# Moving DMA issues, logits order, a split softmax, a one-pass sum and one more tile addition in an attention and MLP kernel

## The chip, the core and the metric

The kernel runs on one core of a Trainium2 chip, in one launch. The metric is the device time of one execution in microseconds, as a median of several runs. A core has five engines with queues of their own: TensorE (PE; its weight loads are listed as PEld), VectorE (DVE), ScalarE (ACT), GpSimd (POOL) and SyncE (SP). Each takes its instructions in order and waits at semaphores. SP, ACT and POOL can issue DMAs, which 16 DMA engines carry out.

## What is computed

x has 2048 rows of 640 in bf16. The output is x plus an attention block plus an MLP, both on the same layer-normalised rows xn. The attention has 32 heads of 20; a row looks at itself and at the seven rows 2, 4, ..., 14 before it.

```python
def _A_ref(x, wqkv, wo):
    H = 32; Dh = D // H
    W, dil = 8, 2
    ...
    logits = jnp.einsum("bhsd,bhswd->bhsw", q, kg) * scale
    logits = jnp.where(mask[None, None, :, :], logits, -1e9)
    attn = _softmax(logits, axis=-1)
    o = jnp.einsum("bhsw,bhswd->bhsd", attn, vg)
    return (lambda x, *d: x.transpose(*d))(o, 0, 2, 1, 3).reshape(B, S, D) @ wo

def _B_ref(x, w1, b1, w2, b2):
    h = jnp.einsum("bsd,df->bsf", x, w1) + b1
    h = _gelu(h)
    return jnp.einsum("bsf,fd->bsd", h, w2) + b2

xn = _layernorm(x, axis=-1)
return x + _A_ref(xn, A_wqkv, A_wo) + _B_ref(xn, B_w1, B_b1, B_w2, B_b2)
```

## The kernel before

The rows are cut into four chunks of 512 (n = 0 to 3, NCH), each of four blocks of 128 (BPC). The 640 columns are five tiles of 128 (KT). Activations are held transposed: 128 columns on the partitions and 512 rows along the free side. The columns of wqkv are taken so that a head's 20 values lie in four neighbouring partitions across all five tiles.

The program is a list of small pieces. ORDER, written out by hand, says in which order they are put into the queues of PE, DVE, ACT and SP; the engines then run apart, held together only by semaphores. A name tells piece and chunk:

- `st`, `su`, `sq`, `rs`, `rc`, `xn`: statistics and normalisation; `tc`: the turn of xn into xnT, for chunks 1 to 3 a DMA transpose issued on SP.
- `pj{n}{which}{to}` and `pc`: projection of q, k or v, five matmuls into one of four psA buffers (L334), and the eviction of that buffer by ACT (L398). Chunk 0 does the same in pairs of blocks (`hj`, `hc`).
- `f1`, `ge`: first MLP product (L586, psA too) and GELU on ACT (L602).
- `qk{n}{pair}{h}`: on DVE, q times the four shifted k of one half h of the window, into the buffer half[h], 5120 elements a partition (L431).
- `pa` and `pb`: on DVE, additions among the five tiles of half[h] (2048 elements each, L463, L468), so that fewer tiles are left for PE. LEVEL[n] says how many: at 0 PE sums five tiles, at 1 tiles 0, 2 and 4, at 2 tiles 0 and 4.
- `lg{n}`: on PE, the sums over the 20 values of a head, one matmul for each tile left, half and block (L477), into the one PSUM tile L.
- `m`, `mx`, `ex`, `ss`, `ri`, `at`: the softmax over the window of eight. Maximum, subtraction, exponential (ACT), sum, reciprocal as exp(-ln) (ACT), product (DVE). ACT needs one table set for GELU and another for exp and ln, and `table` loads it when it changes.
- `xd{n}`, `xs{n}`: the expansion. Four DMAs copy the 32 head rows of each block's attn to the 128 partitions, 256 KB each (L550): blocks 0 and 1 issued on SP (`xd`), 2 and 3 on ACT (`xs`). Chunks 0 and 2 write to the tile ax, 1 and 3 to rows of x_sb that are spent.
- `av{n}{j}{h}`: on DVE, v times the expanded attn of block j, into half[h] (L565). `ad` and `ot` add the window up to oT (L574, L579).
- `t{n}{s}{pc}`: output products of chunks 0 to 2, transposed (L660); `t..4` reads oT. `u` evicts on ACT, `ut` turns the result back by a DMA transpose on SP, `ud` adds it to the output by a DMA from POOL. Chunk 3's products are not transposed (`o`, L621, L623; `o..4` reads oT) and go out by `oc` and `od`. `xp` writes x itself to the output first.
- `ldx`, `ld2`, `ldo`: the later loads on SP (x of chunks 2 and 3, w2, then wo and the broadcast bias b2bc).

The half buffers, L and the softmax tiles exist once. So qk of the next chunk waits until lg has read half, av too, and the next lg waits until the softmax has read L.

Of the kernel before, what the change touches and what calls it, by code (L numbers as in the profile page):

```python
# [30 lines left out]
WARM = 10  # L31
RB = 32
TURNED = 4

LEVEL = (1, 0, 1, 1)
ACT_STATS = (2, 3)

COLS = ((0, 2), (2, 4), (4, 5))

ORDER = """  # L40
pad01 pad02 st00a st00 sum1 rs00 mean1 neg1 sq1 xn00a xn00b tp00a wa tp00b wb tc00a tc00b rs01 ga xn01a xn01b gb2
tp01a gb3 tp01b tc01a tc01b gb4 gd gc0 ge tb b1 gc4 hj100 ho hj101 hj202 st03a st03 st02a st02 gc1 rs03 xn03 hj201
hc100 rs02 xn02 st11a st13a hc202 st10a st11 st12a hc201 tp03 tc03 tp02 tc02 hj200 hc200 hj102 hc102 hc101 hj012 st13
st10 st12 rs1 rc1 hj011 hc011 qk001 hj112 xn10 tc10 hc012 xn12 tc12 qk000 hj111 pa010 hc111 hj110 hc110 pk hc112 hj010
hc010 qk010 qk011 hj211 hc211 pa001 pa011 xn13 tc13 hj210 hc210 xn11 tc11 pa000 f10_10 hj212 hc212 pad12 f10_7 ge0_10
f10_0 f10_4 ge0_4 ge0_7 pad11 f10_6 ge0_6 pj102 pj112 pc102 pj100 ldx ld2 ldo ge0_0 pj103 lg0 mask pc103 pc112 pc100
pj114 su20 pc114 m0 mx0 ex0 pj110 pc110 pj101 pc101 pj111 ss0 pc111 pj113 ri0 at0 xd0 pc113 pj104 pc104 qk100 qk111
qk110 qk101 su21 f10_2 ge0_2 f10_8 ge0_8 xs0 f10_11 ge0_11 f10_1 ge0_1 f11_10 ge1_10 f11_7 ge1_7 f11_3 f11_0 su22
ge1_0 f10_9 f10_3 f10_5 lg1 av030 av020 m1 su23 ge0_9 ng2 sq22 xp0 ge1_3 sq23 ge0_5 sq21 ge0_3 f11_5 ge1_5 av021 sq20
t000 f11_9 ge1_9 rs2 rc2 xn21 tc21 xn20 tc20 mx1 t040 t041 xp1 t001 ex1 av000 pj120 pc120 xn22 tc22 pj122 pc122 av010  # L50
pj124 xn23 tc23 ss1 av011 av001 ri1 at1 xd1 pc124 pj123 av031 ad01 ad00 t042 t002 t003 f11_1 f11_2 pj121 t043 ad02 ot0
su30 pc123 pc121 av101 xs1 av120 av100 pj200 pc200 pj222 av110 av130 pc222 pj221 pc221 pj211 xp2 pc211 pj202 pc202
pj220 av121 pj212 pc220 pc212 pj214 pc214 av131 av111 pj201 pc201 su32 pj204 pc204 pj213 su33 su31 ng3 t004 t044 u00
f11_11 pc213 t010 ut00 t011 sq31 sq30 sq32 u04 sq33 rs3 rc3 t012 t013 t014 pj203 t020 u01 xn30 tc30 pc203 t021 t022
t023 t030 t031 t032 ad10 xn32 tc32 ut01 pj224 t033 ge1_1 xn33 tc33 ad11 ad12 t034 t024 pc224 pj210 xn31 tc31 pc210 ot1
pad21 f11_6 ge1_6 qk201 qk200 f12_4 pa210 ge2_4 ud00 ge1_2 u03 f11_4 ge1_4 pa200 ud01 f11_8 ge1_11 u02 pj302 t120
pj300 pc300 pj311 pc311 pc302 ge1_8 pj312 qk210 pj323 qk211 pa201 pc312 pad22 pj310 pc310 pad31 pa211 pj314 t121 pj301
t122 pc301 pc323 pj303 xl t123 pj304 pj313 lg2 pc313 f13_11 pc314 ut02 ut03 ut04 m2 mx2 pc303 pc304 ge3_11 qk311
f12_10 f12_11 ex2 t100 t101 ss2 ri2 pa311 ud02 at2 f12_7 ge2_10 t102 ge2_7 t124 qk300 t103 t104 xp3 ge2_11 u10 qk310
qk301 pj321 pc321 f13_8 ge3_8 f12_5 ge2_5 pj324 f12_6 xd2 ut10 ud10 pa300 t110 f13_3 t111 t112 pa310 t113 pc324 ge2_6  # L60
f13_0 f12_0 ge3_0 pa301 f12_8 lg3 m3 pj223 u12 ge3_3 mx3 f12_2 xs2 pc223 av201 ex3 t114 u11 ut11 ud11 ss3 ri3 t130
t131 t132 t133 f13_9 t140 t141 t142 ge2_0 av200 at3 ge2_8 av220 av230 xs3 t143 f12_1 ge2_1 t134 ud03 u13 pj320 ge2_2
t144 u14 t200 ut12 av211 av221 av210 av231 ad21 ut13 ad20 ad22 ot2 f13_1 ge3_1 pc320 pj322 pc322 pad32 av331 f12_9
f13_4 ge3_9 f13_5 ge3_5 f12_3 ge2_3 xd3 av311 ut14 f13_6 t201 t230 ud12 xb3 f13_10 t231 ge2_9 t202 t203 ud13 ge3_4
t232 t233 t234 u23 f13_2 t204 u20 ut20 t210 ud14 t211 t212 ud04 av320 f13_7 ud20 t213 ge3_7 t214 t220 t221 ge3_6 u21
t240 av330 t241 t222 t223 t224 t242 t243 u22 ut21 t244 ge3_2 ud21 ut22 ud22 ut23 ud23 o310 o311 o312 av310 ge3_10 o313
av321 av301 av300 ad31 ad30 u24 ut24 ad32 ot3 o320 o321 o322 o323 o324 oc32 o330 od32 o314 oc31 od31 o300 o301 o302
o303 o304 o331 o332 o333 o334 oc30 ohi ud24 oclo ochi ochd od30
""".split()


# [1 line left out]
def kernel(  # L73
# [396 lines left out]
    def do_lg(n):  # L470
        L = psL.tile([P, W, P], F32, tag="L", name="L")
        tiles["L", n] = L
        ts = (range(KT), (0, 2, 4), (0, 4), (0,))[LEVEL[n]]
        for t in ts:
            for h in range(2):
                for j in range(BPC):
                    nc.tensor.matmul(  # L477
                        L[j * H : (j + 1) * H, W // 2 * h : W // 2 * (h + 1), :],
                        lhsT=head_of[:],
                        rhs=half[h][:, :, t, j * P : (j + 1) * P],  # L480
                        start=(t == 0),
                        stop=(t == ts[-1]),
                        skip_group_check=True,
                    )
# [2 lines left out]
        L = tiles["L", 0]  # L487
        nc.vector.tensor_tensor(out=L[0:H, :, 0:MW], in0=L[0:H, :, 0:MW], in1=mask[:], op=ALU.add)

    def do_max(n):  # L490
        m = smp.tile([P, P], F32, tag="m", name="m")
        tiles["m", n] = m
        nc.vector.tensor_reduce(
            out=m[:], in_=tiles["L", n][:].rearrange("p w c -> p c w"), axis=AX.X, op=ALU.max
        )

    def do_sub(n):
        L = tiles["L", n]
        nc.vector.tensor_tensor(  # L499
            out=L[:],  # L500
            in0=L[:],
            in1=tiles["m", n][:].unsqueeze(1).to_broadcast([P, W, P]),
            op=ALU.subtract,
        )

    def do_exp(n):
        e = smp.tile([P, W, P], BF16, tag="e", name="e")
        tiles["e", n] = e
        table(LOG_SET)
        nc.scalar.activation(e[:], tiles["L", n][:], ACT.Exp, scale=SCALE)  # L510

    def do_sum(n):
        a = smp.tile([P, W // 2, P], F32, tag="sums", name="sums")
        tiles["ss", n] = a
        e = tiles["e", n]
        nc.vector.tensor_tensor(out=a[:], in0=e[:, 0 : W // 2, :], in1=e[:, W // 2 :, :], op=ALU.add)
        for k in (2, 1):
            nc.vector.tensor_tensor(out=a[:, 0:k, :], in0=a[:, 0:k, :], in1=a[:, k : 2 * k, :], op=ALU.add)

    def do_recip(n):  # L520
        rs = smp.tile([P, P], F32, tag="m", name="rs")
        tiles["rs", n] = rs
        total = tiles["ss", n][:, 0, :]
        table(LOG_SET)
        nc.scalar.activation(total, total, ACT.Ln)
        nc.scalar.activation(rs[:], total, ACT.Exp, scale=-1.0)

    def do_attn(n):
        attn = smp.tile([P, W, P], BF16, tag="attn", name="attn")
        tiles["attn", n] = attn  # L530
        nc.vector.tensor_tensor(  # L531
            out=attn[:],
            in0=tiles["e", n][:],
            in1=tiles["rs", n][:].unsqueeze(1).to_broadcast([P, W, P]),
            op=ALU.mult,
        )

# [18 lines left out]
        expand(nc.sync, n, (0, 1))  # L556

    def do_xs(n):
        expand(nc.scalar, n, (2, 3))


    def do_av(n, j, h):
# [173 lines left out]
    for n in range(NCH):  # L736
# [30 lines left out]
                piece(f"pb{n}{h}{t}", do_pb, n, h, t)  # L767
        piece(f"lg{n}", do_lg, n)
        for name, fn in (("m", do_max), ("mx", do_sub), ("ex", do_exp), ("ss", do_sum), ("ri", do_recip), ("at", do_attn)):
            piece(f"{name}{n}", fn, n)  # L770
        piece(f"xd{n}", do_xd, n)
        piece(f"xs{n}", do_xs, n)
        for k in range(3):
# [60 lines left out]
```

## Time and profile before

| What | Value |
|---|---|
| time, median of 3 runs | 211.18 us (211.13 to 211.46) |
| the profiled execution: its time | 211.18 us |
| its span in the trace | 209.0 us |
| PE busy | 203.0 us, 1162 matmuls recorded |
| DVE busy | 174.1 us, 141 instructions |
| ACT busy | 124.5 us, 229 instructions |
| POOL busy | 24.8 us |
| mean DMA traffic | 114 GB/s |

The span runs from the program's first instruction to its last; the rest of the time lies around it. Busy time is the union of an engine's instructions. A matmul of 512 columns is listed with 379 ns, but matmuls overlap, and in a row of them one starts every 0.216 us (20 in 4.32 us). "L477" is a line of the kernel. In a group's line the numbers are total busy time, mean ns of one, and the engine's idle time just before, with what ended it. A few matmul records are missing from the trace.

### The profile page before, as it was taken

Reading aid. Unit: us, or ns where it says so; the run is one execution under the profiler, and the core shown is the slowest. Engines: PE = TensorE matmul, PEld = TensorE weight load, DVE = VectorE, ACT = ScalarE, POOL = GpSimd, SP = SyncE. Lnnn points to the kernel's source line nnn. Section 1 sums busy time; section 2 is a strip of 40 time slices with the busy share of each in tenths; the row PEclk is TensorE's granted clock in tenths of the full one; section 3 lists DMA queues with packets and bytes.
Section 4 is the critical chain, followed back from the end, with each engine's and each line's share of the span. In section 5 each row is a group of like instructions: output and inputs, shape, how many; then the busy total and the mean of one; then the engine's idle time right before and its main releaser. Section 6 shows DMA issues by size and latency. Waiting matters only on the chain.

```text
span 209.0 us, 2962 instructions
## 1 busy us (share of the span) xinstructions
PE 203.0 (97%) x1162; PEld 107.1 (51%) x1180; DVE 174.1 (83%) x141; ACT 124.5 (60%) x229; POOL 24.8 (12%) x37
## 2 busy tenths in 40 slices
PE   8999999999999989999999999999999999999993
PEld 3999744544444445444455444444444444445552
DVE  3598996599699999999999879995999999997001
ACT  5579885988988557968765295814756502340210
POOL 2000000000000000020207000202042100225420
PEclk9999999999999999999999999999999999999999
DMA  6994379558006490135719302888189830548633
GB/s 213 387 396 137 68 225 395 226 80 239 13 8 185 79 297 11 25 25 75 104 33 94 25 3 92 127 95 122 32 132 140 80 28 19 56 50 91 56 46 63
DMA packets 36863, 23.88 MB, mean 114 GB/s; under 512 B 24946, under 2 KB 34674, under 8 KB 36850
## 3 DMA queue, kind: packets, MB, share of 16 engines
q1 hardware_dynamic: 25168, 16.65, 29.6%
q0 software_dynamic: 8752, 2.95, 17.5%
q10 hardware_dynamic: 2930, 4.10, 7.4%
q8 instruction: 9, 0.15, 0.3%
q14 instruction: 4, 0.03, 0.1%
HBM read 10.00 MB, written 5.57 MB: 74 GB/s over the span
## 4 chain that ended last, share of the span: by engine, by line
PE 88%; DVE 5%; ACT 2%; DMA 1%; ACTq 1%; issue 1%
PE T L660 24%; PE hps L586 24%; PE pps L334 20%; PE lo L621 7%; PE gps L378 7%; PE L L477 3%; DVE half L565 3%; PE hi L623 2%; PE gps L347 1%; DMA x_sb<-in_A_x_dram 1%; ACTq L550 1%; ACT L171 1%; DVE L L499 1%; DVE attn L531 1%; PE tp L278 0%
## 5 line engine op out<-in xcount | busy, mean ns | idle before, releaser
L586 PE MATMUL hps<-xnT,w_sb 128*128 128x512 bf16 x233 | 54.9, 379 | 0.4
L431 DVE TENSOR_TENSOR half<-qT,kT 128x5120 bf16<-128x5120 bf16 x16 | 44.3, 2818 | 0.0
L660 PE MATMUL T<-hT,w_sb 128*128 128x512 bf16 x179 | 42.7, 379 | 0.1
L672 POOL DMA_DIRECT2D out_dram<-x_sb x15 | 19.4, 1295 | 154.9 <-DMA x_sb<-x_sb 154.6
L586 PEld LDWEIGHTS <-w_sb 128*128 128x128 bf16 x240 | 23.3, 98 | 28.1 <-issue 0.8
L660 PEld LDWEIGHTS <-w_sb 128*128 128x128 bf16 x180 | 17.6, 98 | 21.1
L602 ACT ACTIVATE hT<-hps,bT 128x512 bf16<-128x512 f32 x36 | 23.6, 686 | 6.1 <-PE hps L586 6.0
L565 DVE TENSOR_TENSOR half<-vT,ax 128x2560 bf16<-128x2560 bf16 x16 | 23.1, 1483 | 2.0 <-PE L L477 2.0
L565 DVE TENSOR_TENSOR half<-vT,x_sb 128x2560 bf16<-128x2560 bf16 x16 | 22.6, 1483 | 0.0
L574 DVE TENSOR_TENSOR half<-half,half 128x5120 bf16<-128x5120 bf16 x8 | 22.2, 2822 | 0.1
L334 PE MATMUL pps<-xnT,wv_sb 128*128 128x512 bf16 x73 | 17.9, 379 | 0.9 <-ACT qT L398 0.8
L663 ACT ACTIVATE x_sb<-T,bT 128x512 bf16<-128x512 f32 x15 | 10.3, 685 | 14.0 <-PE T L660 13.0
L334 PE MATMUL pps<-xnT,wq_sb 128*128 128x512 bf16 x75 | 18.3, 379 | 0.0
L660 PE MATMUL T<-oT,wo 128*128 128x512 bf16 x73 | 18.2, 379 | 0.1
L334 PE MATMUL pps<-xnT,wk_sb 128*128 128x512 bf16 x72 | 17.7, 379 | 0.2
L463 DVE TENSOR_TENSOR half<-half 128x2048 bf16<-128x2048 bf16 x12 | 14.1, 1215 | 0.0
L398 ACT CAST qT<-pps 128x512 bf16<-128x512 f32 x15 | 8.7, 590 | 8.9 <-PE pps L334 8.9
L171 ACT ACT_TABLE_LOAD x10 | 12.8, 1283 | 0.9 <-PEq L818 0.7
L261 ACT ACTIVATE xn<-x_sb,nmr,rstd 128x640 bf16<-128x640 bf16 x12 | 11.0, 921 | 3.9 <-DVE nmr L251 2.2
L334 PEld LDWEIGHTS <-wv_sb 128*128 128x128 bf16 x75 | 8.7, 118 | 8.8 <-issue 1.5
L398 ACT CAST kT<-pps 128x512 bf16<-128x512 f32 x15 | 8.7, 587 | 7.3 <-PE pps L334 7.3
L334 PEld LDWEIGHTS <-wq_sb 128*128 128x128 bf16 x75 | 8.8, 117 | 7.5
(90 smaller groups left out, 231.5 us busy)
## 6 DMA issues: line engine op xcount, KB each, us to landing
w_sb<-in_B_w_dram SPq DMA_DIRECT2D x4, 960.0 KB, 10.2
out_dram<-x_sb POOLq DMA_DIRECT2D x15, 128.0 KB, 4.0
x_sb<-in_A_x_dram SPq DMA_DIRECT2D x1, 1280.0 KB, 6.2
out_dram<-x_sb ACTq DMA_DIRECT2D x2, 640.0 KB, 3.8
ax<-attn SPq DMA_DIRECT2D x4, 256.0 KB, 5.9
ax<-attn ACTq DMA_DIRECT2D x4, 256.0 KB, 6.0
x_sb<-attn SPq DMA_DIRECT2D x4, 256.0 KB, 4.7
x_sb<-attn ACTq DMA_DIRECT2D x4, 256.0 KB, 5.1
```

Of the source, the lines that this page charges most:

```text
L171: nc.scalar.preload_act_table_set(name)
L334: nc.tensor.matmul(ps[:], lhsT=wqkv_p[which][:, ti, to, :], rhs=xnT[:, ti, :], start=(ti == 0), stop=(ti == KT - 1),)
L378: nc.tensor.matmul(ps[:, to - a, :], lhsT=wqkv_p[which][:, ti, to, :], rhs=tiles["xnT", 0][:, ti, pair * 2 * P : (pair + 1) * 2 * P], star ...
L398: nc.scalar.copy(dest[:, to, off : off + CH], tiles["pps", n, which, to][:])
L431: nc.vector.tensor_tensor(out=half[h][:, :, :, cs], in0=q[:, :, at].unsqueeze(1).to_broadcast([P, W // 2, KT, 2 * P]), in1=window(k, h, at ...
L565: nc.vector.tensor_tensor(out=half[h][:, :, :, cs], in0=window(qkv_tile(n, 2), h, cs), in1=ax_view(n)[:, j, ws, :].unsqueeze(2).to_broadca ...
L574: nc.vector.tensor_tensor(out=a, in0=a, in1=b, op=ALU.add)
L586: nc.tensor.matmul(ps[:], lhsT=w1_sb[:, ti, ft * P : (ft + 1) * P], rhs=tiles["xnT", n][:, ti, :], start=(ti == 0), stop=(ti == KT - 1),)
L602: nc.scalar.activation(hT, tiles["hps", n, ft][:], ACT.Gelu_apprx_tanh, bias=bT[:, ft : ft + 1], scale=1.0)
L621: nc.tensor.matmul(lo[:], lhsT=lhs, rhs=rhs[:, 0:CH], start=first, stop=last)
L660: nc.tensor.matmul(ps[:], lhsT=lhs, rhs=rhs, start=pc == 0 and k == 0, stop=pc == 4 and k == len(srcs) - 1)
L672: nc.gpsimd.dma_start(dst, src, accum_op=ALU.add)
```

## The change

Five edits and a new ORDER.

- `xs` is issued on SP as well, so all four expansions of a chunk stand on one queue. In ORDER `ldo` and `xp0` come after `xd0` and ahead of `xs0`; in chunks 2 and 3 `xs` comes ahead of `xd`.
- `lg` runs over the halves outside and the tiles inside; it was the other way round.
- PARTS cuts chunk 0's softmax into two parts of 64 columns (`m0a`, `m0b` and so on). The subtraction of a part writes to the first bytes of half[0], in SBUF, not back to L.
- `ss` is one `tensor_reduce` over the window instead of three additions.
- LEVEL is 2 for chunks 2 and 3: two `pb` pieces each, and `lg` over tiles 0 and 4.

ORDER is new as a whole. It is shown where the pieces named here stand.

```diff
--- before.py
+++ after.py
@@ -31,41 +31,43 @@
 WARM = 10
 RB = 32
 TURNED = 4
-
-LEVEL = (1, 0, 1, 1)
+PARTS = (2, 1, 1, 1)
+
+LEVEL = (1, 0, 2, 2)
 ACT_STATS = (2, 3)
 
 COLS = ((0, 2), (2, 4), (4, 5))
 
 ORDER = """
...
-f10_0 f10_4 ge0_4 ge0_7 pad11 f10_6 ge0_6 pj102 pj112 pc102 pj100 ldx ld2 ldo ge0_0 pj103 lg0 mask pc103 pc112 pc100
-pj114 su20 pc114 m0 mx0 ex0 pj110 pc110 pj101 pc101 pj111 ss0 pc111 pj113 ri0 at0 xd0 pc113 pj104 pc104 qk100 qk111
-qk110 qk101 su21 f10_2 ge0_2 f10_8 ge0_8 xs0 f10_11 ge0_11 f10_1 ge0_1 f11_10 ge1_10 f11_7 ge1_7 f11_3 f11_0 su22
...
-pj124 xn23 tc23 ss1 av011 av001 ri1 at1 xd1 pc124 pj123 av031 ad01 ad00 t042 t002 t003 f11_1 f11_2 pj121 t043 ad02 ot0
-su30 pc123 pc121 av101 xs1 av120 av100 pj200 pc200 pj222 av110 av130 pc222 pj221 pc221 pj211 xp2 pc211 pj202 pc202
...
-t122 pc301 pc323 pj303 xl t123 pj304 pj313 lg2 pc313 f13_11 pc314 ut02 ut03 ut04 m2 mx2 pc303 pc304 ge3_11 qk311
-f12_10 f12_11 ex2 t100 t101 ss2 ri2 pa311 ud02 at2 f12_7 ge2_10 t102 ge2_7 t124 qk300 t103 t104 xp3 ge2_11 u10 qk310
-qk301 pj321 pc321 f13_8 ge3_8 f12_5 ge2_5 pj324 f12_6 xd2 ut10 ud10 pa300 t110 f13_3 t111 t112 pa310 t113 pc324 ge2_6
-f13_0 f12_0 ge3_0 pa301 f12_8 lg3 m3 pj223 u12 ge3_3 mx3 f12_2 xs2 pc223 av201 ex3 t114 u11 ut11 ud11 ss3 ri3 t130
...
+pj113 pc113 pj103 pj111 ge0_10 pj101 pc111 pj114 ldx ge0_7 pa000 pc101 pa010 lg0 mask m0a ld2 pc103 pj102 pc114 pad11
+su21 mx0a ex0a pj112 pc112 m0b mx0b ss0a pc102 ex0b ri0a ss0b pj100 pc100 at0a ri0b at0b pj110 pj104 pc104 pc110 xd0
+qk111 f10_2 ge0_2 su22 qk100 hj212 hc212 f10_6 ge0_6 pj121 su20 f10_1 pc121 su23 ldo f11_10 ge1_10 ng2 ge0_1 sq20
+f11_5 f10_11 pj122 pc122 f10_3 qk110 sq22 t040 qk101 f11_0 t000 lg1 xp0 av010 ge0_3 sq21 xs0 ge1_0 sq23 rs2 f10_8
+ge0_8 t001 m1 f11_3 rc2 xn23 tc23 ge0_11 av031 t041 mx1 av021 xn20 tc20 f11_7 av011 ge1_5 ge1_7 av001 ge1_3 xp1 f10_9
+t042 t002 xn21 ge0_9 tc21 pj120 xn22 tc22 av030 av000 f11_9 ge1_9 pj124 ex1 av020 ss1 pc120 pc124 pj123 pc123 ad00 ri1
+t043 f11_2 t003 pj204 at1 pc204 xd1 su31 ad01 pad12 ad02 ot0 pj200 pc200 pj201 pc201 av101 xp2 pj212 su30 pc212 pj220
...
+pj302 pc302 f13_6 ge3_6 pj323 lg2 pc312 qk300 m2 pc323 f11_11 ge1_11 f13_0 ge3_0 mx2 ut04 f13_11 ge3_9 ex2 pa300 ss2
+qk310 ri2 at2 xs2 qk301 t130 t131 f12_1 ge2_1 ge3_11 t132 f13_10 qk311 t102 t103 f13_2 pa310 xd2 t104 pj320 pc320
+f13_1 ge3_1 u10 ut10 ud10 f12_8 pa311 pa301 pb312 ge2_8 f13_8 ge3_8 t110 t133 t111 t112 t113 t114 u11 ge3_10 f12_5
+pj222 pc222 pj321 pc321 pb302 lg3 av200 t134 u13 m3 av221 ge2_5 xb3 f12_11 t140 t141 t120 ut11 mx3 f12_2 ge3_2 av211
...
 """.split()
@@ -471,8 +473,8 @@
         L = psL.tile([P, W, P], F32, tag="L", name="L")
         tiles["L", n] = L
         ts = (range(KT), (0, 2, 4), (0, 4), (0,))[LEVEL[n]]
-        for t in ts:
-            for h in range(2):
+        for h in range(2):
+            for t in ts:
                 for j in range(BPC):
                     nc.tensor.matmul(
                         L[j * H : (j + 1) * H, W // 2 * h : W // 2 * (h + 1), :],
@@ -487,51 +489,62 @@
         L = tiles["L", 0]
         nc.vector.tensor_tensor(out=L[0:H, :, 0:MW], in0=L[0:H, :, 0:MW], in1=mask[:], op=ALU.add)
 
-    def do_max(n):
-        m = smp.tile([P, P], F32, tag="m", name="m")
-        tiles["m", n] = m
+
+    def part(n, i):
+        width = P // PARTS[n]
+        return slice(i * width, (i + 1) * width), width
+
+    def softmax_tile(key, n, shape, dtype):
+        return get((key, n), lambda: smp.tile([P, PARTS[n]] + [s // PARTS[n] if s == P else s for s in shape], dtype, tag=key, name=key))
+
+    def shifted(n, i):
+        cs, width = part(n, i)
+        if PARTS[n] == 1:
+            return tiles["L", n][:]
+        low = half[0][:].rearrange("p w t c -> p (w t c)").bitcast(F32)[:, 0 : W * P]
+        return low.rearrange("p (i w c) -> p i w c", i=PARTS[n], w=W)[:, i, :, :]
+
+    def do_max(n, i):
+        cs, width = part(n, i)
+        m = softmax_tile("m", n, [P], F32)
         nc.vector.tensor_reduce(
-            out=m[:], in_=tiles["L", n][:].rearrange("p w c -> p c w"), axis=AX.X, op=ALU.max
-        )
-
-    def do_sub(n):
-        L = tiles["L", n]
+            out=m[:, i, :], in_=tiles["L", n][:, :, cs].rearrange("p w c -> p c w"), axis=AX.X, op=ALU.max
+        )
+
+    def do_sub(n, i):
+        cs, width = part(n, i)
         nc.vector.tensor_tensor(
-            out=L[:],
-            in0=L[:],
-            in1=tiles["m", n][:].unsqueeze(1).to_broadcast([P, W, P]),
+            out=shifted(n, i),
+            in0=tiles["L", n][:, :, cs],
+            in1=tiles["m", n][:, i, :].unsqueeze(1).to_broadcast([P, W, width]),
             op=ALU.subtract,
         )
 
-    def do_exp(n):
-        e = smp.tile([P, W, P], BF16, tag="e", name="e")
-        tiles["e", n] = e
+    def do_exp(n, i):
+        e = softmax_tile("e", n, [W, P], BF16)
         table(LOG_SET)
-        nc.scalar.activation(e[:], tiles["L", n][:], ACT.Exp, scale=SCALE)
-
-    def do_sum(n):
-        a = smp.tile([P, W // 2, P], F32, tag="sums", name="sums")
-        tiles["ss", n] = a
-        e = tiles["e", n]
-        nc.vector.tensor_tensor(out=a[:], in0=e[:, 0 : W // 2, :], in1=e[:, W // 2 :, :], op=ALU.add)
-        for k in (2, 1):
-            nc.vector.tensor_tensor(out=a[:, 0:k, :], in0=a[:, 0:k, :], in1=a[:, k : 2 * k, :], op=ALU.add)
-
-    def do_recip(n):
-        rs = smp.tile([P, P], F32, tag="m", name="rs")
-        tiles["rs", n] = rs
-        total = tiles["ss", n][:, 0, :]
+        nc.scalar.activation(e[:, i, :, :], shifted(n, i), ACT.Exp, scale=SCALE)
+
+    def do_sum(n, i):
+        total = softmax_tile("sums", n, [P], F32)
+        nc.vector.tensor_reduce(
+            out=total[:, i, :], in_=tiles["e", n][:, i, :, :].rearrange("p w c -> p c w"), axis=AX.X, op=ALU.add
+        )
+
+    def do_recip(n, i):
+        rs = get(("rs", n), lambda: smp.tile([P, PARTS[n], P // PARTS[n]], F32, tag="m", name="rs"))
+        total = tiles["sums", n][:, i, :]
         table(LOG_SET)
         nc.scalar.activation(total, total, ACT.Ln)
-        nc.scalar.activation(rs[:], total, ACT.Exp, scale=-1.0)
-
-    def do_attn(n):
-        attn = smp.tile([P, W, P], BF16, tag="attn", name="attn")
-        tiles["attn", n] = attn
+        nc.scalar.activation(rs[:, i, :], total, ACT.Exp, scale=-1.0)
+
+    def do_attn(n, i):
+        cs, width = part(n, i)
+        attn = get(("attn", n), lambda: smp.tile([P, W, P], BF16, tag="attn", name="attn"))
         nc.vector.tensor_tensor(
-            out=attn[:],
-            in0=tiles["e", n][:],
-            in1=tiles["rs", n][:].unsqueeze(1).to_broadcast([P, W, P]),
+            out=attn[:, :, cs],
+            in0=tiles["e", n][:, i, :, :],
+            in1=tiles["rs", n][:, i, :].unsqueeze(1).to_broadcast([P, W, width]),
             op=ALU.mult,
         )
 
@@ -556,7 +569,7 @@
         expand(nc.sync, n, (0, 1))
 
     def do_xs(n):
-        expand(nc.scalar, n, (2, 3))
+        expand(nc.sync, n, (2, 3))
 
 
     def do_av(n, j, h):
@@ -767,7 +780,8 @@
                 piece(f"pb{n}{h}{t}", do_pb, n, h, t)
         piece(f"lg{n}", do_lg, n)
         for name, fn in (("m", do_max), ("mx", do_sub), ("ex", do_exp), ("ss", do_sum), ("ri", do_recip), ("at", do_attn)):
-            piece(f"{name}{n}", fn, n)
+            for i in range(PARTS[n]):
+                piece(f"{name}{n}" + ("" if PARTS[n] == 1 else "ab"[i]), fn, n, i)
         piece(f"xd{n}", do_xd, n)
         piece(f"xs{n}", do_xs, n)
         for k in range(3):
```

## The prediction

> **What bounds the kernel now.** I read the page first (busy shares, 40 slices, the chain that ended last), then PE's waits, the chain in order of time around each logits block, the timeline around PE's one wait, and VectorE's groups with the shapes kept apart.
>
> ```profile
> PE 203.0 (97%) x1162; PEld 107.1 (51%) x1180; DVE 174.1 (83%) x141; ACT 124.5 (60%) x229; POOL 24.8 (12%) x37
> PEclk9999999999999999999999999999999999999999
> DMA  6994379558006490135719302888189830548633
> PE 88%; DVE 5%; ACT 2%; DMA 1%; ACTq 1%; issue 1%
> ```
>
> PE is busy 97% of the span at full granted clock, and 88% of the last chain is PE. Its matmuls start 0.216 us apart (20 hps matmuls in 4.32 us on the chain), so this is work, not waiting. A change pays only if it takes matmuls away from PE or closes a hole in PE, and it costs only where it opens one. There is one hole after the start:
>
> ```profile
> PE pps L334 <- ACT qT L398: 0.8, 1, 0.8
> ```
>
> That is PE's list of waits; its place in the timeline (start, us, engine, line; idle before it in brackets):
>
> ```profile
> 70.86 2.36 ACTq L550 DMA_DIRECT2D x_sb<-attn  x2
> 73.26 0.59 ACT L398 CAST qT<-pps 128x512 bf16<-128x512 f32 x1 [2.39 <-PE pps L334]
> 73.89 0.59 PE L334 MATMUL pps<-xnT,wv_sb 128*128 128x512 bf16 x2 [0.85 <-ACT qT L398]
> ```
>
> At 70.86 ScalarE issues chunk 1's two expansions (xs1) and cannot get past them until 73.22. The q eviction behind them is late, its accumulator buffer is not free, and PE stands still for 0.8 us.
>
> ```profile
> 53.62 2.27 PE L L477 x40
> ...
> 142.91 1.41 PE L L477 x24
> ```
>
> These are chain pieces: start, us, line, count. Chunk 1's 40 logits matmuls (five tiles) and chunk 3's 24 (three tiles).
>
> ```profile
> L463 DVE TENSOR_TENSOR half<-half 128x2048 bf16<-128x2048 bf16 x12 | 14.1, 1215 | 0.0
> L493 DVE TENSOR_REDUCE m<-L 128x128 f32<-128x1024 f32 x4 | 4.9, 1223 | 4.6 <-PE L L477 4.5
> L516 DVE TENSOR_TENSOR sums<-e 128x512 f32<-128x512 bf16 x4 | 2.8, 688 | 1.6 <-ACT e L510 1.6
> L518 DVE TENSOR_TENSOR sums<-sums 128x256 f32<-128x256 f32 x4 | 1.7, 426 | 0.1
> L518 DVE TENSOR_TENSOR sums<-sums 128x128 f32<-128x128 f32 x4 | 1.2, 292 | 0.1
> ```
>
> VectorE (83%) is second. Between the first products (17.7) and the last oT (192.3) it waits only around the logits and the softmax. So the question is whether VectorE, with more to do, still delivers before PE asks.
>
> **The change part by part.** The profiled execution took 211.18 us: 209.0 span and 2.18 around it. It is also the median, so the sum starts there.
>
> *One tile more added (LEVEL 2 in chunks 2 and 3).* PE loses 2 x 8 = 16 logits matmuls. From the two pieces above one costs (2.27 - 1.41)/16 = 0.054 us, four running side by side. **-0.86 us**, all on PE's path. VectorE gains four pb additions of 2048 elements, which L463 prices at 1.215 us, 1.14 from start to start: +4.5 us, hidden or not as below.
>
> *Expansions all from SyncE.* Eight issues leave ScalarE. Six of them hold up nobody on PE; the pair at 70.86 makes the hole: **-0.8 us**, back to zero at best. On SP's queue they now stand: in chunk 0 behind wo, b2bc and the residual write xp0; in chunk 1 right behind xd1, ahead of ut00 and the last four xnT transposes; in chunks 2 and 3 ahead of xd, with two ut transposes between in chunk 3. An issue on SP took 0.6 us, 1.7 at worst, so what stands behind them is 1 to 3 us later; xn's transposes in chunk 3 are issued some 20 us after xs1, and the ut transposes feed only output writes. I cost that at nothing. Expansions landing late are a rival below. Two pairs on one queue landed 1.8 and 2.2 us apart, so four should be in about 9.5 us after the first issue; chunk 1's fourth is wanted by the fourth av, after two ad, oT and three av: 2.85 + 2.85 + 1.4 + 4.2 = 11.3 us after at1.
>
> *Logits half by half.* The same matmuls in another order, nothing on PE. Half 0 is free after half of the block, so VectorE starts earlier by 0.4 us (chunks 2, 3) to 1.1 us (chunk 1).
>
> *Chunk 0's softmax in two column parts.* Four more VectorE instructions; 512-element ones cost 0.69 (L516) against 1.22 for 1024, so 2 x 0.69 - 1.22 = 0.16 each, +0.6 us. In return the waits of 1.33 us for the exponential and 0.72 for the reciprocal are overlapped by the other part. The subtraction writes to half 0 in SBUF, so the q·k product into half 0 waits for both exponentials; half 1's product stands ahead of it. Net: attn about 1 us earlier. PE is not there to gain by it.
>
> *Exponentials summed in one pass.* Three additions (0.69 + 0.43 + 0.29 = 1.41) become one reduce of 1024 to 128. No row shows it on SBUF data with the summed elements 256 bytes apart. Lower bound: the max reduce over the same 1024 elements, in PSUM, 1.22. Upper bound: one lost cycle for every element; a cycle from 512 to 1024 elements is (1.22 - 0.69)/512 = 1.04 ns, so 1.22 + 1.07 = 2.29. I take the middle, 1.75, not the low end: PE's weight loads that step through SBUF in strides of five elements took 118 ns (L334), contiguous ones 98 (L586), so spread reads from SBUF are not free. Against 1.22 that is +0.53 a chunk. [...] By the PSUM row alone, 1.22, the time is 209.6.
>
> *Whether VectorE delivers.* I counted the changed ORDER between the points where both meet. Steps from start to start: product 2.74, av 1.40, tile addition 1.14, max 1.14 to 1.26, subtraction and attn 1.14, ad 2.74 to 2.85.
> - lg2 to lg3. PE: 16 x 0.054 + 0.19 at the block's edges + 105 matmuls x 0.216 = 23.7. VectorE starts 0.7 after lg2 does, so it has 23.0. It has four products (10.96), four pa and two pb (6.84), max, subtraction, attn (3.54) and the sum (1.14 as a 1.22 reduce): 22.5. Free: about 0.4. With the reduce at 1.75 it is 0.1 over, and with the edges I put **+0.2** on PE.
> - lg1 to t004, which needs oT0. PE: 2.4 + 118 x 0.216 = 27.9, less 1.3 before VectorE starts = 26.5. VectorE: eight av (11.2), max, subtraction, attn, nmr (3.5), three ad and oT (9.9), sum 1.14: 25.8. Free 0.65; at 1.75, 0.1.
> - lg3 to t204 (oT2). PE: 1.06 + 114 x 0.216 + six lo/hi pairs x 0.27 = 27.3, less 0.7 = 26.6; VectorE the same list without nmr, 25.7. Free 0.8; at 1.75, 0.3. Chunk 3's av then have some 0.9 to spare before o324.
> The two close ones get **+0.1** more together.
>
> *ScalarE* loads its function tables 12 times, not 10: +2 x 1.28 us, covered by ScalarE's 40% idle. Without that cover 1.28 each. The other moves in ORDER keep PE's and ScalarE's instructions and shift who evicts which of the four psA buffers when. The smallest waits listed for PE are 0.2 (transposes on xn); half of one, **+0.1**, is what I put for new ones.
>
> Sum: 211.18 - 0.86 - 0.8 + 0.2 + 0.1 + 0.1 = **209.9 us**. A measurement of this kernel tells about 0.2%, 0.42 us, from no change.
>
> **The rivals.**
> 1. *The reduce pays a full cycle per element (2.29).* lg3 is then late by 1.07 - 0.4 = 0.65, t004 by 0.4, t204 by 0.3: 1.35 in place of 0.3, so 211.0, no change. For it: no spread SBUF read on VectorE in the trace. Against: L493's stride costs nothing. [...]
> 2. *Chunk 0's expansions land late: slower.* Place: the av of block 3 is the second after lg1, at about 57.1 in the changed order, and block 3 is last on one queue behind two expansions, wo, b2bc and xp0, the first issued at about 41.8. That leaves 15.3 us. Before, four expansions and xp0 (1664 KB) took 42.79 to 54.70, 11.9 us; wo and b2bc are 960 KB. At the pace of the weight loads (4000 KB in 13.2 us) they add 3.2, 15.1 in all, just in time; at the pace of that stretch (140 KB/us) 6.9, which is 3.5 late. With 0.1 free at t004 nearly all of it reaches PE: 213.3. It decides from 0.2 us late on; 1.7 late makes the change a loss. Against: the DMA row has its engines at 5 and 8 tenths in the slices from 41.8 to 52.3 and at 0 in the next, so there is room for 3 us of loads.
> 3. *PE's hole only moves.* Evictions pile up behind a table load or another wait, and PE loses 0.8 as before: 210.7. For it: two more table loads, and 60% of ScalarE's time is taken. Against: in the whole trace this happened once, behind two DMA issues that are now gone.
>
> **How the numbers follow.** Forecast 0.62, rival 1 0.13, rival 2 0.14, rival 3 0.11. Faster: forecast and rival 3, 0.73. Same: rival 1 for the most part, 0.12. Slower: rival 2 and rival 1's far end, 0.15. Range: below, 211.18 - 1.66 with none of the three additions, less the 0.3 us by which the runs of before differ (211.13 to 211.46), 209.2; above, rivals 3 and 1 and the near part of rival 2, to 211.6.
>
> **What would show it.** L logits pieces of 16 in about 0.97 us for chunks 2 and 3; no PE wait for a q eviction of 0.8; no expansion on ACT's queue; the sums reduce near 1.75 us (1.22 or 2.29 move the time to 209.6 or 211.0); VectorE ending pb302 just ahead of lg3. The prediction is wrong if PE waits over 0.5 us in one place, above all T or L for VectorE, or if VectorE's first av wait for ax.

## The result and the profile after

The changed kernel takes 210.07 us (median of 11 runs, 209.83 to 211.51); the kernel before, run beside it, 211.84 us (11 runs, 211.02 to 213.02). The ratio is 0.993, with a 95% interval of 0.9907 to 0.9954: faster by 0.7%. On another chip, beside two experiments, it was 209.92 us, ratio 0.9918 (0.9887 to 0.9949). The prediction was 209.9 us. The ratios leave out the few executions that ran at a lower granted clock (0.984 to 0.992), which the medians and ranges below keep (up to 218.67 us).

The forecast started from the median of three runs of before, 211.18 us, and so stood for -1.28 us, a ratio of 0.994. By eleven runs the kernel before is at 211.84, but the lowest runs are 1.19 us apart (211.02 and 209.83). The profiled execution took 210.03 us with a span of 208.0, against 211.18 and 209.0 before, 1.15 us less; the terms of the sum are compared on this pair.

The page of the changed kernel, the lines that answer to the first fence of before:

```profile
PE 203.5 (98%) x1164; PEld 107.0 (51%) x1164; DVE 180.9 (87%) x141; ACT 127.5 (61%) x234; POOL 24.9 (12%) x37
...
PEclk9999999999999999999999999999999999999999
DMA  6994379168426075148431790086405795556753
...
PE 66%; DVE 21%; ACT 9%; DMA 2%; issue 1%; DVEq 0%; ACTq 0%
```

The granted clock is full in both (1.000 before, 0.999 after). VectorE has 6.8 us more to do, and the last line is what matters: before, 88% of the chain that ended last was PE's own work; now 21% of it is VectorE. PE's busy share has not fallen, but at some joints PE now follows VectorE. PE's list of waits names two of them (us in total, times, longest), where before it named one of 0.8 us for a q eviction:

```profile
PE T L673 <- DVE oT L592: 0.3, 1, 0.3
PE L L479 <- DVE half L470: 0.2, 1, 0.2
```

The first is t004 at 81.86 us, the second lg3 at 145.22. A third stop is not in the list, because only 0.09 us of it lie behind the modelled end of the matmul before. It shows between the starts of two hps matmuls, at 156.57 and 157.04: 0.47 us apart, 0.25 more than usual. The late one waits for an accumulator that ScalarE has to empty. ScalarE's timeline there (start, us; idle before it in brackets):

```profile
154.34 0.31 ACT L538 ACTIVATE sums<-sums 128x128 f32<-128x128 f32 x1 [2.19 <-DVE sums L530]
154.68 0.31 ACT L539 ACTIVATE rs<-sums 128x128 f32<-128x128 f32 x1
155.00 1.28 ACT L173 ACT_TABLE_LOAD   x1
156.30 1.84 ACT L615 ACTIVATE hT<-hps,bT 128x512 bf16<-128x512 f32 x3
```

ScalarE stands 2.19 us for chunk 3's sum, then needs the logarithm, the exponential and a table load of 1.28 before its next GELU; three GELUs have piled up by then (x3).

The place of the old hole, in the timeline of all engines:

```profile
72.75 0.58 ACT L400 CAST qT<-pps 128x512 bf16<-128x512 f32 x1
...
73.22 0.59 ACT L400 CAST qT<-pps 128x512 bf16<-128x512 f32 x1
...
73.87 1.24 PE L336 MATMUL pps<-xnT,wv_sb 128*128 128x512 bf16 x5
...
74.71 2.44 SPq L563 DMA_DIRECT2D x_sb<-attn  x3
```

The q evictions now follow each other, PE's v product stands without a bracket, and the expansions are issued by SyncE (SPq) at 74.71. VectorE's groups with the shapes kept apart:

```profile
L530 DVE TENSOR_REDUCE sums<-e 128x128 f32<-128x1024 bf16 x3 | 5.8, 1917 | 0.3 <-ACT e L526 0.3
...
L510 DVE TENSOR_REDUCE m<-L 128x128 f32<-128x1024 f32 x3 | 3.7, 1218 | 0.0
...
L530 DVE TENSOR_REDUCE sums<-e 128x64 f32<-128x512 bf16 x2 | 2.1, 1057 | 0.0
```

The new sum (L530) takes 1.917 us for 1024 elements, where the maximum over as many (L510) takes 1.218. The bracket of 0.3 us is chunk 1's sum waiting for its exponential.

To add PE up I take the trace's starts of the matmuls. From the first product of the opening (5.97 us before, 6.25 after; over all traces here it lies between 5.97 and 7.18) to the last matmul's start (205.65 and 204.59) PE takes 199.68 us before and 198.34 after: -1.33. Four terms make up most of it.

- -0.86 for the 16 logits matmuls.
- -1.02 for the hole at 73.
- -0.28 for a smaller hole in the opening, which the new order closes. The first product behind the last transposes there started 0.33 us after the last of them, and now starts 0.06 after it. The chain that ended last goes through ScalarE's v eviction there before (the first two lines), and through PE alone after (the last two):

```profile
13.40 0.59 ACT vT L393
14.04 9.44 PE gps L378 x85
...
13.54 0.56 PE tp L280 x10
14.10 9.28 PE gps L380 x85
```

- +0.93 of new stops: 0.44 at t004 (0.66 from the start of the matmul before, where 0.22 is usual), 0.24 at lg3 (0.55, where the step into a logits block is 0.31 when nothing waits) and 0.25 at 157.04.

That is -1.23; the other -0.10 lies in steps too small to name.

### The profile page after: what moved, and what is told of

Its sections match the earlier page's. It is cut to its first block, busy times and chain, and to the rows that moved or that the text cites. A ratio compares the mean times of both kernels' runs of the same rounds, so it can differ in the third digit from the quotient of the medians.

```text
span 208.0 us, 2951 instructions
## 1 busy us (share of the span) xinstructions
PE 203.5 (98%) x1164; PEld 107.0 (51%) x1164; DVE 180.9 (87%) x141; ACT 127.5 (61%) x234; POOL 24.9 (12%) x37
## 4 chain that ended last, share of the span: by engine, by line
PE 66%; DVE 21%; ACT 9%; DMA 2%; issue 1%; DVEq 0%; ACTq 0%
PE T L673 17%; PE pps L336 15%; PE hps L599 13%; PE lo L634 7%; PE gps L380 7%; DVE half L433 5%; DVE half L587 4%; DVE sums L530 3%; PE idle L446 2%; ACT L173 2%; DVE half L465 2%; DMA xnT<-xn 2%; DVE half L578 2%; ACT hT L615 2%; PE hi L636 2%; PE gps L349 1%
## 5 line engine op out<-in xcount | busy, mean ns | idle before, releaser
L599 PE MATMUL hps<-xnT,w_sb 128*128 128x512 bf16 x240 | 56.9, 379 | 0.1
L673 PE MATMUL T<-hT,w_sb 128*128 128x512 bf16 x180 | 43.3, 379 | 0.0
L615 ACT ACTIVATE hT<-hps,bT 128x512 bf16<-128x512 f32 x36 | 24.1, 687 | 7.3 <-PE hps L599 7.2
L336 PE MATMUL pps<-xnT,wk_sb 128*128 128x512 bf16 x75 | 18.3, 379 | 0.0
L336 PEld LDWEIGHTS <-wk_sb 128*128 128x128 bf16 x75 | 8.8, 117 | 7.5
L400 ACT CAST vT<-pps 128x512 bf16<-128x512 f32 x15 | 8.5, 589 | 6.1 <-PE pps L336 6.1
```

Of the source, the lines that this page charges most:

```text
L336: nc.tensor.matmul(ps[:], lhsT=wqkv_p[which][:, ti, to, :], rhs=xnT[:, ti, :], start=(ti == 0), stop=(ti == KT - 1),)
L599: nc.tensor.matmul(ps[:], lhsT=w1_sb[:, ti, ft * P : (ft + 1) * P], rhs=tiles["xnT", n][:, ti, :], start=(ti == 0), stop=(ti == KT - 1),)
L615: nc.scalar.activation(hT, tiles["hps", n, ft][:], ACT.Gelu_apprx_tanh, bias=bT[:, ft : ft + 1], scale=1.0)
L673: nc.tensor.matmul(ps[:], lhsT=lhs, rhs=rhs, start=pc == 0 and k == 0, stop=pc == 4 and k == len(srcs) - 1)
```

## The experiments

### The sum over neighbouring elements

```diff
 def do_sum(n, i):
     total = softmax_tile("sums", n, [P], F32)
-    nc.vector.tensor_reduce(
-        out=total[:, i, :], in_=tiles["e", n][:, i, :, :].rearrange("p w c -> p c w"), axis=AX.X, op=ALU.add
-    )
+    e = tiles["e", n][:, i, :, :]
+    terms = e.rearrange("p w c -> p (w c)").rearrange("p (c w) -> p c w", w=W) if n else e.rearrange("p w c -> p c w")
+    nc.vector.tensor_reduce(out=total[:, i, :], in_=terms, axis=AX.X, op=ALU.add)
```

> The changed kernel, but in chunks 1 to 3 the one-pass sum reads eight neighbouring bf16 elements instead of eight that lie 256 bytes apart (so those sums are over the wrong exponentials; the number of elements and the output are the same; chunk 0 is as it was). Theory A, spread reads are what the reduce pays for: the three 1024-element sums drop from 1.92 us to about the 1.22 us of the max reduce, VectorE is 0.7 us earlier at each joint, PE's small waits at t004 (0.44 us), lg3 (0.24 us) and the ScalarE one near 156.6 us (0.25 us) go, and the time falls by 0.7 to 0.9 us, to 209.1 to 209.4. Rival B, the price belongs to the bf16 source in SBUF or to the reduce as such and not to the spread: the sums stay at 1.9 us, the waits stay, and the time is that of the changed kernel within 0.2 us.

Measured: 209.28 us (9 runs, 208.95 to 211.72), ratio to before 0.9902 (0.9871 to 0.9934); PE's stretch from first product to last start is 197.53 us, 0.81 below the changed kernel; from the first logits block to the last start, with the opening left out, it is 169.56 against 170.49, 0.93 below. The sum in VectorE's groups:

```profile
L532 DVE TENSOR_REDUCE sums<-e 128x128 f32<-128x1024 bf16 x3 | 3.7, 1218 | 0.2 <-ACT e L526 0.2
```

1.218 us, what the maximum over PSUM takes, from the same bf16 tile in SBUF by the same instruction. So theory A holds, and rival B falls: the 0.70 us belong to the 256-byte steps. All three stops of PE are gone (the starts there are 0.22 us apart again, and 0.31 at lg3), and behind the opening PE gains the 0.93 us that they came to. With the sum at 1.218 us, PE does not wait anywhere behind the opening: the new stops are the price of the spread reads.

### The three additions put back

```diff
-    nc.vector.tensor_reduce(... axis=AX.X, op=ALU.add)
+    nc.vector.tensor_tensor(out=a[:, i], in0=e[:, i, 0 : W // 2, :], in1=e[:, i, W // 2 :, :], op=ALU.add)
+    for k in (2, 1):
+        nc.vector.tensor_tensor(out=a[:, i, 0:k, :], in0=a[:, i, 0:k, :], in1=a[:, i, k : 2 * k, :], op=ALU.add)
```

> The changed kernel with the old three additions in place of the one-pass sum, all else as changed. Theory A, the reduce is a loss: three additions take about 1.4 us from start to start against 1.85 us for the reduce, VectorE is some 0.4 us earlier at each of lg3, t004 and t204, PE's waits there shrink from 0.44 and 0.24 us to 0 to 0.1 us, and the time is 0.4 to 0.8 us below the changed kernel. Rival B, PE's waits hang on something else (the accumulator buffers, ScalarE): the time is the changed kernel's within 0.2 us, though VectorE is earlier. Rival C, three instructions cost more than they show (two more starts in the queue, each waiting for the one before): slower than the changed kernel.

Measured: 209.35 us (6 runs, 209.02 to 210.17), ratio 0.9903 (0.9876 to 0.9929), span of the profiled run 207.0. VectorE's groups of the sum for chunks 1 to 3, the first addition, the third and the second (the third's group counts two of chunk 0's as well):

```profile
L532 DVE TENSOR_TENSOR sums<-e 128x512 f32<-128x512 bf16 x3 | 2.1, 690 | 0.3 <-ACT e L526 0.3
...
L534 DVE TENSOR_TENSOR sums<-sums 128x128 f32<-128x128 f32 x5 | 1.5, 291 | 0.2
...
L534 DVE TENSOR_TENSOR sums<-sums 128x256 f32<-128x256 f32 x3 | 1.3, 425 | 0.1
```

0.69 + 0.43 + 0.29 = 1.41 us against 1.917. PE's stretch is 197.45 us, 0.89 below the changed kernel, and 0.93 below it from the first logits block on; no PE wait for VectorE or ScalarE is left after the opening. Theory A holds: by the median (0.72 us below, on another chip) inside its range, by PE's stretch a little beyond the upper end. The third rival, that more instructions cost more, falls. So one of the five edits is a loss, and the kernel without it is the fastest found here that computes the reference. I ran that version again beside the changed kernel on one chip:

> The changed kernel with the three additions again, as candidate for the fastest version, beside the changed kernel on one chip. If the one-pass sum is what opens PE's 0.93 us of small waits, it is 0.8 to 1.0 us below the changed kernel here too, near 209.1 us; if the earlier difference was one between chips, the two are within 0.3 us.

> The changed kernel once more, beside the next two on one chip: 209.8 to 210.1 us, 0.993 of before. Nothing else is told apart by it.

Measured: 209.39 us (6 runs, 209.04 to 210.3), ratio 0.9898 (0.9864 to 0.9933), beside 209.92 us (6 runs, 209.76 to 210.22) for the changed kernel. The medians differ by 0.53 us and the lowest runs by 0.72. That lies between my two cases; the intervals of the two ratios overlap, so the times alone would not settle it. The traces do: the changed kernel again has its three stops (0.36, 0.24 and 0.24 us), the other none, and from the first logits block on they take 170.39 and 169.56 us. The profiled run with the three additions lost 0.8 us to a late first weight load instead, which no edit touches.

### One part alone: expansions from SyncE in the kernel before

```diff
 def do_xs(n):
-    expand(nc.scalar, n, (2, 3))
+    expand(nc.sync, n, (2, 3))
```

> The kernel before with one part of the change alone: blocks 2 and 3 of the expansion are issued on SyncE instead of ScalarE, at the same place in the order. Theory A: PE's 0.8 us wait for a q eviction at about 73.9 us goes, nothing new comes, and the time falls by 0.8 us (0.4%). Rival B, the hole only moves or a later joint has the same slack: PE waits elsewhere and the time is within 0.2 us of before. Rival C, the expansions land late on one queue: VectorE waits for ax in an av and PE for oT, slower by 1 us or more. SyncE issues chunk 0's second pair here behind the weight wo.

Measured: 210.68 us (12 runs, 210.21 to 213.99), ratio 0.9954 (0.9928 to 0.9979). The timeline at the place of the hole:

```profile
71.27 3.79 SPq L550 DMA_DIRECT2D x_sb<-attn  x4
...
72.21 2.32 PE L334 MATMUL pps<-xnT,wv_sb 128*128 128x512 bf16 x10
```

Ten v products run through while SyncE issues all four expansions. PE's stretch is 198.66 us against 199.68 before: -1.02, and the list of waits has nothing in the hole's place. Theory A holds; the hole did not move. It was larger than the 0.8 us that the list of waits gave: between the starts of the matmuls it is 1.01 us, since the list counts only from the modelled end of the matmul before.

### Another part alone: two tile additions more in the old order

```diff
-LEVEL = (1, 0, 1, 1)
+LEVEL = (1, 0, 2, 2)
 ORDER = """
-... pj310 pc310 pad31 pa211 pj314 ...
+... pj310 pc310 pad31 pa211 pb212 pb202 pj314 ...
-... f13_0 f12_0 ge3_0 pa301 f12_8 lg3 ...
+... f13_0 f12_0 ge3_0 pa301 pb312 pb302 f12_8 lg3 ...
```

> The kernel before with another part alone: two more tile additions on VectorE in chunks 2 and 3, put right behind the last of the others, 16 logits matmuls fewer on PE, the rest of the order as it was. Theory A, VectorE has little to spare between the joints of the old order: each pair of additions costs VectorE 2.28 us, less than 1 us of which is free, so PE waits at lg2 and lg3 some 1.8 to 2.5 us each where it waited at nothing; the time rises by 2.5 to 3.5 us in spite of the 0.86 us of matmuls saved. Rival B, VectorE's waits around the logits (2.1 and 2.4 us in the trace of before) absorb them: the time falls by 0.9 us.

Measured: 213.69 us (6 runs, 213.14 to 218.67), ratio 1.0092 (1.0065 to 1.0119). PE's list of waits:

```profile
PE L L477 <- DVE half L468: 2.8, 2, 1.4
...
PE pps L334 <- ACT qT L398: 0.8, 1, 0.8
...
```

PE waits 1.4 us at each of lg2 and lg3 (1.46 by the starts). 2 x 1.46 - 0.86 = 2.1 us, and the lowest runs are 2.0 apart (213.14, and 211.15 of the kernel before on that chip). Theory A was right on the sign and the places, and too high on the size: I expected 1.8 to 2.5 us at each joint, and VectorE had 2.28 - 1.46 = 0.8 us free in front of it. Rival B falls: VectorE's waits around the logits came behind PE and could not be moved ahead of it. Taken alone, the edit that saves PE 0.86 us makes the kernel 0.9% slower. What turns it in the whole change can be counted between lg2 and lg3. VectorE has the same list there in both kernels, but PE has 105 other matmuls in the changed one and 99 here, which is 1.30 us more of its own work in front of lg3. VectorE starts 0.71 us after lg2 does and not 1.10, and its list takes 23.23 us and not 22.76, for the slower sum above all. 1.46 - 1.30 - 0.39 + 0.47 = 0.24 us, the stop that the changed kernel has at lg3. So the larger part comes from where the new ORDER puts PE's work; no run here changes that alone.

### Chunk 0's softmax in one part

```diff
-PARTS = (2, 1, 1, 1)
+PARTS = (1, 1, 1, 1)
 (m0, mx0, ex0, ss0, ri0 and at0 stand once each in ORDER)
```

> The changed kernel with chunk 0's softmax in one part again (PARTS 1 for all chunks; each piece at the place of its first or last half; the subtraction writes back to L). Theory A, the split is off PE's path: attn and the four expansions come about 1 us later, block 3's expansion still lands ahead of its av (it had 1.6 us to spare), and the time is the changed kernel's within 0.2 us. Rival B, the split also paces ScalarE: with the exponential of all 1024 elements and its wait in one piece, the evictions of the projections behind it come late and PE waits 0.3 to 0.5 us near 40 us; slower by that.

Measured: 210.44 us (6 runs, 210.34 to 210.95), ratio 0.9951 (0.9932 to 0.997), span of the profiled run 208.5 against 208.0. The joints with VectorE are as in the changed kernel (0.42, 0.23, 0.25), but PE has two new gaps, 0.23 us at 39.65 and 0.27 at 44.75. ScalarE's timeline there:

```profile
38.55 1.02 ACT L526 ACTIVATE e<-L 128x1024 bf16<-128x1024 f32 x1 [1.57 <-DVE L L516]
39.47 0.58 ACT L400 CAST kT<-pps 128x512 bf16<-128x512 f32 x1
39.94 1.09 ACT L400 CAST qT<-pps 128x512 bf16<-128x512 f32 x2
...
43.20 1.28 ACT L173 ACT_TABLE_LOAD   x1
44.50 0.69 ACT L615 ACTIVATE hT<-hps,bT 128x512 bf16<-128x512 f32 x1
```

ScalarE waits 1.57 us for the whole subtraction and only then empties accumulators, k at 39.47; everything to the GELU at 44.50 is a microsecond later (43.53 in the changed kernel). Rival B holds: the split paces ScalarE, and PE gains 0.5 us by it. This is shown for the pieces at these places of ORDER; an order written for one part might hide it.

### Logits with the tiles outside again

```diff
-        for h in range(2):
-            for t in ts:
+        for t in ts:
+            for h in range(2):
```

> The changed kernel with the logits loop back to tiles outside and halves inside; the same matmuls. Theory A, half by half buys VectorE its early start and nothing is free behind it: the first av after lg1 starts 1.0 us later, the first q times k product or av after lg2 and lg3 0.4 us later; t004's wait on PE grows from 0.44 to 0.9 to 1.4 us, lg3's from 0.24 to 0.5 to 0.7 us; the time rises by 1.0 to 1.7 us over the changed kernel. Rival B, the order of the logits is off the path: within 0.2 us of the changed kernel.

Measured: 210.98 us (12 runs, 210.76 to 212.39), ratio 0.9988 (0.9968 to 1.0009): no different from before. PE's list of waits:

```profile
...
PE T L673 <- DVE oT L592: 0.8, 1, 0.8
PE L L479 <- DVE half L470: 0.3, 1, 0.3
PE hps L599 <- ACT hT L615: 0.3, 1, 0.3
```

The first av after lg1, in the changed kernel and here:

```profile
54.97 1.49 DVE L578 TENSOR_TENSOR half<-vT,ax 128x2560 bf16<-128x2560 bf16 x1 [1.69 <-PE L L479]
...
56.02 1.49 DVE L578 TENSOR_TENSOR half<-vT,ax 128x2560 bf16<-128x2560 bf16 x1 [2.55 <-PE L L479]
```

It starts 1.05 us later in the trace, but lg1 itself starts 0.19 later here; from lg1's start it is 2.16 us instead of 1.30, so the loop order costs VectorE 0.86 us. Behind lg2 and lg3 it is 0.21. t004's stop grows by 0.49 us, lg3's by 0.12, the one near 157 by 0.20. Together that is 0.81 us at the joints, 1.08 between the profiled executions (211.11 and 210.03), where some 0.3 lies in the opening: theory A's mechanism and places, with delays and time a little below its lower end. Rival B falls. A loop order that moves no work and costs PE nothing was worth almost as much as the 16 matmuls.

### Without the tile more

```diff
-LEVEL = (1, 0, 2, 2)
+LEVEL = (1, 0, 1, 1)
 (pb212, pb202, pb312 and pb302 left out of ORDER)
```

> The changed kernel without its one tile more: LEVEL 1 in chunks 2 and 3, the four pb additions left out, all else in place. PE gets 16 logits matmuls more (0.86 us), VectorE loses 2.28 us of work a chunk. Theory A: PE's small waits at lg3 (0.24 us) and near 156.6 us (0.25 us) go, the one at t004 (0.44 us), which lies ahead of these chunks, stays; the time rises by 0.86 - 0.49, about 0.4 us, so in this kernel the edit is worth half of what its matmuls are. Rival B, the waits have another cause and stay: 0.86 us up. Rival C, the additions cost as much as they bring: no change within 0.1 us.

Measured: 210.52 us (12 runs, 210.27 to 211.66), ratio 0.9955 (0.9929 to 0.9981); profiled 210.44 against 210.03. PE's stretch is 198.86 us, 0.51 above the changed kernel, of which 0.11 lies in the opening. PE keeps one wait, 0.3 us at t004, and the stops at lg3 and 157 are gone, as theory A has it: 0.86 - 0.49 = 0.37 expected, 0.40 measured from the first logits block on. In the finished change the edit keeps about half of its 0.86 us; the other half goes back through the joints with VectorE.

### More ahead of chunk 0's expansions

Two doses: the residual write of chunk 1, then those of chunks 1 and 2 (640 KB each), on SyncE ahead of xs0.

```diff
-        (nc.scalar if n else nc.sync).dma_start(dst, x_sb[:, cs, :])
+        (nc.scalar if n > 1 else nc.sync).dma_start(dst, x_sb[:, cs, :])   # second dose: n > 2
 ORDER = """
-... lg1 xp0 av010 ge0_3 sq21 xs0 ... ge1_3 xp1 f10_9 ... av101 xp2 pj212 ...
+... lg1 xp0 xp1 av010 ge0_3 sq21 xs0 ... ge1_3 f10_9 ...              # second dose: xp0 xp1 xp2
```

> The changed kernel with the residual write of chunk 1 (640 KB) moved from ScalarE's queue to SyncE's, right behind that of chunk 0 and so ahead of chunk 0's expansions of blocks 2 and 3. Theory A, the queue's order is what decides when an expansion lands: 640 KB more ahead of them cost 2.75 us (the time between the landings of the bias and of the first residual write) to 4.6 us (140 KB/us), of which 1.6 us were spare; VectorE's av of block 3 waits 1.1 to 3 us for ax, t004 waits as much longer, and the time rises by 1.0 to 3 us. Rival B, the 16 DMA engines have room and work on both at once: the expansions land within 1.6 us of where they did and the time is unchanged within 0.2 us.

Measured: 210.22 us (12 runs, 209.86 to 211.79), ratio 0.9942 (0.9916 to 0.9968), the changed kernel's. Block 3's expansion landed 15.61 us after the first issue, 1.67 us later than in the changed kernel (13.94). With the write ahead of it on the queue it lands later, as theory A says, but 640 KB cost less than the 2.75 us that I gave them. The 1.67 is one pair of traces, and without the write block 3 landed 13.18 to 14.48 us after the first issue in eight traces. The landings on the queue itself agree better: the second write landed 1.58 us after the first. The 1.6 us to spare were just enough: block 3 landed at 58.34 and VectorE's av starts at 58.36 with no wait. Theory A's mechanism holds and its price does not. t004's stop of 0.44 us is down to 0.09 here. In the changed kernel the residual write on ScalarE's queue, at 60.69, overlaps an xnT transpose on SyncE that lands 4.2 us after its issue instead of 2.4; ScalarE's xn, the exponential behind it and chunk 1's sum (0.25 us) wait for that:

```profile
60.69 4.22 DMA xnT<-xn
65.00 0.92 ACT xn L263
```

These are pieces of the chain that ended last in the changed kernel. With the write elsewhere, the sum does not wait.

> The changed kernel with the residual writes of chunks 1 and 2 (640 KB each) on SyncE's queue ahead of chunk 0's expansions of blocks 2 and 3. One of them put block 3's landing 1.67 us later after the first issue, which was all that it had to spare. Theory A, the late expansion reaches PE undiminished: block 3 lands another 1.5 to 1.8 us later, VectorE waits that long for ax ahead of the second av, PE at t004 1.2 to 1.7 us, and the time rises by 1.2 to 1.7 us over the changed kernel (0.3 us less if the residual write's leaving ScalarE brings t004 its old 0.3 us back). Rival B, something downstream has room and takes it: PE waits under 0.5 us at t004.

Measured: 211.47 us (12 runs, 211.07 to 212.05), ratio 0.9994 (0.9974 to 1.0015), 1.55 us above the changed kernel on the same chip. The lists of waits, VectorE and PE:

```profile
DVE half L578 <- DMA ax<-attn: 1.3, 1, 1.3
...
PE T L673 <- DVE oT L592: 0.8, 1, 0.8
```

The writes landed 1.58 and 1.59 us apart. Block 3 landed 17.01 us after the first issue, another 1.40 later, and now an av waits 1.33 us for ax. PE loses it in two portions: 0.59 us at 72.68 and 74.08, because ScalarE waits 2.24 us for chunk 1's sum with the q evictions queued behind it, and 0.57 more at t004 than the changed kernel on that chip. Together 1.16 us of 1.33; PE's stretch is 1.18 us longer than the changed kernel's on that chip. Theory A holds, and rival B falls: the expansion was late, and nearly all of it reached PE.

## Why the prediction was right, point by point

**What bounds the kernel**: held. PE's stretch follows its matmuls and its stops in every trace above. There were two holes before and not one, though: the smaller, 0.28 us in the opening, was overlooked.

**One tile more, -0.86 us**: right. 16 matmuls take 0.98 us from the block's first start to the next instruction's, 24 take 1.41: 0.43 a chunk. The pb additions cost 1.219 us each (L470), as priced (1.215).

**Expansions from SyncE, -0.8 us**: the mechanism was right, alone and in the whole; the size was 1.02. The step that was short took the list of waits' 0.8, where the gap between matmul starts is 1.01. No transfer came up on PE's path for standing behind the expansions on SyncE; the one late transpose, at 60.69, was late beside a write from ScalarE.

**The one-pass sum**: 1.917 us, above the middle of 1.75 that I took and inside the bounds. By the experiment with neighbouring elements the 256-byte steps cost (1.917 - 1.218) us / 1024 = 0.68 ns an element, 0.66 of the 1.04 ns that an element adds by the rows of before. The three additions put back show that the edit itself is a loss: 0.5 us per chunk on VectorE and 0.93 on PE. I priced it above the additions, 1.75 against 1.41, and still let the edit stand as +0.3 among the joints.

**The joints, +0.2 at lg3, +0.1 more at t004 and t204, +0.1 elsewhere**: 0.24, 0.44 at t004 with none at t204, and 0.25 (at 157.04): 0.93 in place of 0.4. lg3 was counted right: 0.1 over by the tally, and 0.24 with a sum 0.17 us longer. At t004 the tally left out a wait of VectorE, the 0.25 us for the exponential. The stop at 157.04 is one that I said would not be: the table load at 155.00 is not covered by ScalarE's idle 40%, since it comes behind a wait for the sum and ahead of GELUs that PE needs. Idle time on average is no cover at a place.

**The split softmax, nothing on PE**: wrong. It is worth 0.5 us, by way of ScalarE's queue. I had looked for its effect through attn and the expansions only, and the new ORDER would have opened that gap without it.

**Half by half, an earlier start for VectorE**: right in the mechanism, smaller in size (0.86 us for chunk 1 where I had 1.1, 0.21 for chunks 2 and 3 where I had 0.4), and worth 0.8 us at PE's joints, which my sum holds only inside the tallies.

**Rival 1 (a full cycle lost)**: the reduce lost 0.68 ns an element, 0.66 of the 1.04 that I called a cycle. **Rival 2 (late expansions)**: in the changed kernel block 3 landed 13.94 us after the first issue, at 55.95, and its av began at 57.58; I had 15.1 and 15.3. The pace of 140 KB/us, from which the 6.9 us came, was far off; writes of 640 KB on that queue landed 1.58 us apart, 405 KB/us. The mechanism and its price, 1.16 us of PE for 1.33 late, were shown by the second dose. **Rival 3 (the hole moves)**: it did not in the part alone; in the whole, the 0.25 us at 157.04 is a small case of it.

So that the sum was right to 0.15 us is luck: two errors cancel. The gains were short by 0.50 us (0.22 at the hole, 0.28 at the one overlooked in the opening), the losses by 0.53. With both put right the sum is 209.95 us. The profiled execution took 210.03: its first product started 0.27 us later than in that of before, PE saved the 0.10 us not named above, and 0.10 us less lies around the span.

## What to carry to other kernels

Count the second engine between the points where it meets the first, and count its waits in with its work: the same two additions a chunk cost 2.1 us in one order and earn 0.4 in another, and what decided, by the count between two logits blocks, was 1.3 us more of the first engine's work in between and a start of the second 0.4 us earlier. Price a reduce by the step between the elements that it reads as well as by their number: 1024 of them took 1.917 us here at steps of 256 bytes and 1.218 as neighbours, and three passes over contiguous data, 1.41 us, beat the one over spread data. And take a hole's size from the starts of the instructions around it, since the list of waits counted 0.8 of 1.0.

## What was not expected of the hardware

- A one-pass sum on VectorE over bf16 elements 256 bytes apart in SBUF took 1.917 us for 1024 of them, over neighbouring ones 1.218; with 128-byte steps 1.057 us for 512, where the maximum over 512 elements in PSUM took 0.69. The maximum over 1024 elements of f32 in PSUM with 512-byte steps took 1.218 too, and the subtraction over the same 1024 in order 1.228: the steps cost nothing there.
- Residual writes of 640 KB, issued one behind another on one DMA queue with loads and expansions around them, landed 1.58, 1.58 and 1.59 us apart (405 KB/us).
- A transpose by DMA landed 4.2 us after its issue, instead of 2.4, when a 640 KB write was issued on another queue at the same time. All eight traces of kernels with that write show it (4.16 to 4.25 us). In the two doses, which have the write elsewhere, no transpose of that group with a recorded landing took over 2.48. In the kernel before, a transpose issued 0.94 us after the write took 3.02.
